# Two of the seven gate and value products, in the last two chunks, done as seven products of blocks of 128

## The chip, the cores and the metric

The kernel runs on one core of a Trainium2 chip. The metric is the device time of one execution in microseconds, as the median of several runs. One execution was also recorded by the hardware profiler; its times are measured from the start of its span.

## The reference

Attention with a threshold, followed by a SwiGLU block, all in float32. There are 8 batches of 8 heads, 576 positions, 64 columns a head.

```python
scores = scale * np.matmul(q, k.transpose(0, 1, 3, 2))
thresh = np.max(scores, axis=-1, keepdims=True) - tau
scores = np.where(scores >= thresh, scores, -1000000000.0)
attn = exp(scores - max); attn = attn / (sum(attn) + 1e-09)
x = (attn @ v) as (4608 tokens, 512)
g = x @ w_gate                       # 512 x 1536
silu = g * (1.0 / (1.0 + np.exp(-g)))
val = x @ w_val                      # 512 x 1536
return (silu * val @ w_out)          # 1536 x 512
```

## The kernel before

**Tokens and chunks.** The SwiGLU block works on chunks of 512 tokens. Chunks 0 to 7 are the first 512 positions of each batch, chunk 8 is the last 64 positions of all batches together. While the attention of batch c + 1 runs, its scores and softmax take turns with the SwiGLU steps of chunk c. After the last scores nothing is left but the end of chunk 6's output and chunks 7 and 8; this part is called the tail (`tail[0]` is true, L1833). There the sums that GpSimd does otherwise are VectorE's, and the four PSUM banks of the scores join the other four (`more_banks`, L1837).

**A group.** Gate and value of a chunk are made in 6 groups (g = 0 to 5) of 256 gate and 256 value columns. A group is one product of a 2 x 2 matrix of weight blocks by a 2 x 2 matrix of token blocks, each block 256 x 256: the halves of the inner dimension, gate against value, the two halves of the tokens. It is done with seven block products instead of eight, with sums and differences of blocks. Class `Group` (L923) has a method for each product, p1 to p7. Each calls `mul` (L935), four matmuls of 128x128 stationary weights by 128x256 tokens. They collect in the banks pa, pb and pe; ScalarE copies a bank between two products, or moves it to SBUF halved (L947, L963, L984, L1015). In p3, VectorE makes the first gate from pe and what ScalarE put aside (L1005); `finish` (L988) then has ScalarE make a tanh (L992) and VectorE two more steps (L993, and L798 for the last multiplication). `gates_and_values` (L1702) runs the groups; the order on TensorE is p1 of a group, p4 of the group before, then p5, p2, p6, p3, p7.

**Weights.** Sums of weights that were made early lie in HBM. For chunks from 2 on, each group's seven weight blocks come into one of two places in SBUF (`flow`, slot g % 2) in two loads, `load_flow` (L866 to L875): blocks 0 to 3 (1024 KB) and 4 to 6 (768 KB). The loads for group g + 2 are issued at the end of p6 (first part) and p4 (second part) of group g. Block 2 belongs to p5, block 5 to p3.

**Tokens.** `token_sums` (L888) makes the sums of token blocks. xs[0] is p5's, xs[2] is p3's.

**The output stage.** `Deep` (L1239) does the product with w_out in blocks, again with seven products. Its `nested` (L1302) splits five of them once more, each into seven products of three matmuls, 128x128 by 128x128, whose results lie in blocks of two banks in the order ORDER and at the places AT (L1299, L1300). Its sums are VectorE's in the tail (L798, shapes 128x512 and 128x384). `early` and part of the inner sums are made during groups 4 and 5, the rest while the stage runs. `combine` (L1338) adds the seven blocks into four, four adds in a row, from SBUF or from PSUM.

**The order of work.** A planner in the kernel's own code, class `Plan` (L28), fixes the order in which every engine gets its instructions. Each step is a job with an engine, an expected cost, the jobs it depends on, and a rank; TensorE's order is written out by hand, and the planner hands out the other engines' jobs in the order in which they would start. Once built, each engine's queue is strictly in that order, so an instruction that waits holds up all behind it.

Of the kernel before, what the change touches and what calls it, by code (L numbers as in the profile page):

```python
# [27 lines left out]
class Plan:  # L28
# [84 lines left out]
def kernel(  # L113
# [656 lines left out]
    def take(name, full=False):  # L770
        free = [b for b in banks if (not b.held if b.fixed is not None else b.n in turns)]
        if full:
            free = [b for b in free if b.full]
            return Hold(min(free, key=Bank.free_at), name) if free else None
        n = sum(b.full for b in free)
        return Hold(min(free, key=lambda b: (b.full and n == 1, max(b.free_at(), plan.t))), name)
# [20 lines left out]
    def dve_tt(out, a, b, op):  # L797
        return lambda: nc.vector.tensor_tensor(out=out, in0=a, in1=b, op=op)  # L798
# [89 lines left out]
    def token_sums(c, c2, deps, eng="POOL"):  # L888

        x11, x12, x21, x22 = (x_block(c, t, kh)[:, c2] for t in range(2) for kh in range(2))  # L890
        s1, s2, s4 = (x[:, c2] for x in xs)
        tt, took = (pool_tt, 0.75) if eng == "POOL" else (dve_tt, 0.36)
        j1 = job(eng, took, tt(s1, x21, x22, ALU.add), *deps, rank=0)
        j2 = job(eng, took, tt(s2, s1, x11, ALU.subtract), j1, rank=0)
        j4 = job(eng, took, tt(s4, x12, s2, ALU.subtract), j2, rank=0)
        j3 = job(eng, took, tt(x21, x11, x21, ALU.subtract), j1, rank=0)
        jobs = ready_x.setdefault(c, {n: [] for n in range(5)})
        for n, j in ((1, j1), (2, j2), (3, j3), (4, j4)):
            jobs[n].append(j)
        jobs[0] += deps  # L900
# [22 lines left out]
    class Group:  # L923
# [78 lines left out]
        def p3(self):  # L1002
            m = self.mul(self.e, self.w[5], xs[2], False, self.s5, *self.w_deps[5], *ready_x[self.c][4])
            u = self.u1_buf
            g1 = job("DVE", 0.7, lambda: nc.vector.scalar_tensor_tensor(out=u.ap, in0=self.e.rows(), scalar=0.5, in1=u.ap, op0=ALU.mult,  # L1005
                                                                        op1=ALU.add), m, self.u1, rank=0)
            self.e.read_by(g1)
            self.e.done(True)
            self.finish(0, u, g1, self.a, self.m2)
# [10 lines left out]
        def p4(self):  # L1020
            m = self.mul(self.b, self.w[4], x_block(self.c, 1, 1), False, self.u2, *self.w_deps[4])
            self.finish(1, self.u2_buf, self.g2, self.b, m)
            if self.g + 2 < NF2:
                if self.c < DEEP:
                    load_sums(self.c, self.g + 2, m)
                else:
                    load_flow(self.c, self.g + 2, 1, m)

    def plain_group(t, g, n_bufs):

        x = xts["full", t]

        def mul(mat, name):
            hold = take(name)

            def fn():
                ps = hold.rows()
                for i in range(2):
                    for c in range(NCC):
                        nc.tensor.matmul(ps[:, i], wgv[:, mat, c, (2 * g + i) * P:(2 * g + i + 1) * P], x[:, c, :],  # L1040
                                         start=(c == 0), stop=(c == NCC - 1))
# [197 lines left out]
    class Deep:  # L1239
# [62 lines left out]
        def nested(self, o, holds, first, *deps):  # L1302

            ws = weights_of(o)
            begun = set() if first else {0, 1}
            for n in self.ORDER:
                a, ready = self.inner[o][n]
                bank_, at_ = self.AT[n]

                def fn(n=n, a=a, bank_=bank_, at_=at_):  # L1310
                    ps = holds[bank_].ap()[:, at_ * P:(at_ + 1) * P]
                    for f in range(NF2 // 2):
                        nc.tensor.matmul(ps, a[:, f, :], ws[n][:, f, :], start=bank_ not in begun, stop=True, skip_group_check=True)  # L1313
                        begun.add(bank_)

                m = pe(0.67, fn, *ready, *deps, *deep_jobs[o])
            return m
# [384 lines left out]
    def gates_and_values(c):  # L1702

        old = None
        while u_bufs[0] is not u_list[0]:
            u_bufs.rotate(-1)
        for g in range(NF2):
            new = Group(c, g)
            new.p1(tail[0] or g not in (2, 4))
            yield  # L1710
            if old is not None:
                old.p4()
                if c >= DEEP and old.g == NF2 - 2:
# [12 lines left out]
        state["last_product"] = old.p4  # L1726
# [110 lines left out]
    def more_banks():  # L1837
        plan.force(*sc_users)
        for _ in range(2):
            ps = ps_s.tile([P, 2, 512], F32, name="sc")  # L1840
            for h in range(2):
                b_ = Bank(None, ps[:, h])
                banks.append(b_)

    more_banks()
    while state["run"]:
        out_steps(1)
    for c in (B - 1, B):
        for _ in gates_and_values(c):
            pass  # L1850
        begin_outputs(c)
        out_steps(2)
        if c < B:
            w = SM // 2
            j = []
            for kh in range(2):
                src = last_hbm[:, 2 * kh:2 * kh + 2, :].rearrange("p c (t n) -> p t c n", t=2)
                for t in range(2):
                    j.append(job("SP", 0.1, lambda kh=kh, t=t, src=src: nc.sync.dma_start(out=x_place(B, kh)[:, t], in_=src[:, t]),
                                 last_store[0], plan.t, lag=3.0))  # L1860
            for c2 in range(2):
                token_sums(B, c2, j, "DVE")
        while state["run"]:
            out_steps(1)
    plan.finish()


# [28 lines left out]
```

## Time and profile before

| | |
|---|---|
| median of 3 runs | 1383.91 us (1381.97 to 1387.38) |
| profiled execution | 1383.97 us |
| its span | 1382.1 us |
| granted TensorE clock, mean | 0.998 |
| busy over the span: PE, PEld, DVE | 1360.9 (98%), 1115.3 (81%), 1024.5 (74%) |
| busy over the span: ACT, POOL | 867.6 (63%), 701.2 (51%) |
| end of the last scores | 1141.5 us |
| first product of chunk 7, of chunk 8 | 1165.60, 1271.93 us |

The profile names an engine as PE (TensorE's matmuls), PEld (its weight loads), DVE (VectorE), ACT (ScalarE), POOL (GpSimd) or SP (SyncE, which issues the DMAs). A row shows the line of the code, what is written and read, the shape, and in brackets how long the engine stood idle before it and what released it. L798 is a helper that all two-operand sums on VectorE go through, L940 the matmuls of a group, L1313 the narrow ones of the output stage, L1322 its wide ones. The durations of matmuls overlap, so their pace is read from start to start.

### The profile page before, as it was taken

Reading aid. Unit: us, or ns where it says so; the run is one execution under the profiler, and the core shown is the slowest. Engines: PE = TensorE matmul, PEld = TensorE weight load, DVE = VectorE, ACT = ScalarE, POOL = GpSimd, SP = SyncE. Lnnn points to the kernel's source line nnn. Section 1 sums busy time; section 2 is a strip of 40 time slices with the busy share of each in tenths; the row PEclk is TensorE's granted clock in tenths of the full one; section 3 lists DMA queues with packets and bytes.
Section 4 is the critical chain, followed back from the end, with each engine's and each line's share of the span. In section 5 each row is a group of like instructions: output and inputs, shape, how many; then the busy total and the mean of one; then the engine's idle time right before and its main releaser. Section 6 shows DMA issues by size and latency. Waiting matters only on the chain.

```text
span 1382.1 us, 38805 instructions
## 1 busy us (share of the span) xinstructions
PE 1360.9 (98%) x15486; PEld 1115.3 (81%) x15486; DVE 1024.5 (74%) x2677; ACT 867.6 (63%) x2254; POOL 701.2 (51%) x649
## 2 busy tenths in 40 slices
PE   9988999999999999999999999999999999999998
PEld 6666787777778778887888888878887788889888
DVE  7978888887887777787778877877787764366355
ACT  6887766676755767767776766776767773220320
POOL 2456498844484669533974387437943592000000
PEclk9999999999999999999999999999999999999999
DMA  7733413465514541555154523553165404424411
GB/s 172 212 104 138 102 36 96 120 189 143 176 47 126 142 114 42 169 143 142 35 152 129 151 50 126 138 141 93 36 190 143 112 26 142 153 77 145 153 61 31
DMA packets 208291, 162.29 MB, mean 117 GB/s; under 512 B 166128, under 2 KB 180464, under 8 KB 202736
## 3 DMA queue, kind: packets, MB, share of 16 engines
q1 hardware_dynamic: 203920, 158.86, 40.7%
q8 instruction: 123, 2.02, 0.6%
q10 hardware_dynamic: 4192, 0.95, 0.3%
q14 instruction: 56, 0.46, 0.1%
HBM read 138.28 MB, written 21.50 MB: 116 GB/s over the span
## 4 chain that ended last, share of the span: by engine, by line
PE 91%; DVE 4%; ACT 2%; SPq 1%; DMA 1%; issue 1%; ACTq 0%; DVEq 0%
PE pb L940 17%; PE pa L940 12%; PE pe L940 12%; PE px L1313 12%; PE sc L1545 10%; PE xa L1642 9%; PE po L1109 5%; PE py L1322 5%; PE pg L1040 2%; PE pv L1040 2%; PE sc L940 1%; PE pv L517 1%; SPq L336 1%; PE xa L500 1%; PE sc L1313 1%
## 5 line engine op out<-in xcount | busy, mean ns | idle before, releaser
L1593 DVE SCALAR_TENSOR_TENSOR pall<-sc,th,pall 128x288 f32<-128x288 f32 x504 | 243.8, 514 | 63.6 <-ACT pall L1591 49.4
L940 PE MATMUL pb<-xall,big 128*128 128x256 f32 x1080 | 256.5, 380 | 0.0
L1591 ACT ACTIVATE pall<-sc,nm 128x288 f32<-128x288 f32 x504 | 232.0, 498 | 34.5 <-DVE pall L1593 34.2
L1621 DVE STREAM_TRANSPOSE pall<-pall 128x576 f32<-128x576 f32 x252 | 190.0, 765 | 59.4 <-ACT pall L1619 42.7
L940 PEld LDWEIGHTS pb<-xall,big 128*128 128x128 f32 x1080 | 203.7, 190 | 29.8 <-issue 2.2
L1619 ACT ACTIVATE pall<-pall,ri 128x288 f32<-128x288 f32 x408 | 186.8, 528 | 24.9 <-DVE ri L1607 24.3
L795 POOL TENSOR_TENSOR hall<-hall,tmp 128x512 f32<-128x512 f32 x80 | 103.7, 1296 | 160.2 <-DVE hall L993 144.8
L940 PE MATMUL pa<-xall,big 128*128 128x256 f32 x768 | 183.3, 381 | 0.0
L940 PE MATMUL pe<-xall,big 128*128 128x256 f32 x752 | 178.9, 381 | 0.0
L940 PEld LDWEIGHTS pa<-xall,big 128*128 128x128 f32 x768 | 144.0, 190 | 22.6 <-issue 2.7
L940 PEld LDWEIGHTS pe<-xall,big 128*128 128x128 f32 x752 | 141.9, 190 | 21.5 <-issue 2.7
L1545 PE MATMUL sc<-kT,qT 64*32 64x144 f32 (+1 forms) x5376 | 149.0, 345 | 3.4 <-DVE pall L1593 2.3
L1566 DVE TENSOR_REDUCE mx<-sc 128x2 f32<-128x576 f32 x168 | 124.8, 743 | 26.7 <-PE sc L1545 26.1
L1545 PEld LDWEIGHTS sc<-kT,qT 64*32 64x32 f32 x5376 | 97.5, 106 | 57.1 <-issue 21.1
L1642 PE MATMUL xa<-pall,vall 64*32 64x288 f32 x4032 | 132.2, 404 | 1.1 <-DVE hall L993 0.8
L1616 POOL TENSOR_SCALAR pall<-pall,ri 128x288 f32<-128x288 f32 x96 | 95.9, 1010 | 62.5 <-DVE ri L1607 62.4
L1642 PEld LDWEIGHTS xa<-pall,vall 64*32 64x32 f32 x4032 | 76.4, 107 | 50.2 <-issue 7.3
L1601 ACT COPY sums<-sums 32x6 f32<-32x6 f32 x336 | 66.7, 199 | 45.0 <-DVE pall L1593 40.5
L992 ACT ACTIVATE vall<-tmp 128x512 f32<-128x512 f32 x96 | 60.5, 630 | 52.6 <-DVE tmp L1005 29.9
L1580 ACT COPY mx<-mx 32x6 f32<-32x6 f32 x196 | 38.1, 195 | 61.3 <-DVE mx L1568 59.3
L1322 PE MATMUL py<-wo,hall 128*128 128x256 f32 x336 | 74.8, 379 | 0.0
L1568 DVE TENSOR_REDUCE mx<-sc 128x1 f32<-128x288 f32 x168 | 74.7, 445 | 0.0
(231 smaller groups left out, 2327.1 us busy)
## 6 DMA issues: line engine op xcount, KB each, us to landing
big<-sums_hbm SPq DMA_DIRECT2D x42, 1024.0 KB, 5.2
big<-sums_hbm SPq DMA_DIRECT2D x48, 768.0 KB, 4.8
vall<-in_v_dram SPq DMA_DIRECT2D x112, 144.0 KB, 3.0
out_dram<-big SPq DMA_DIRECT2D x32, 256.0 KB, 3.1
qT<-in_q_dram SPq DMA_DIRECT2D x112, 72.0 KB, 4.7
kT<-in_k_dram SPq DMA_DIRECT2D x112, 72.0 KB, 3.1
wo<-in_moe_w_gate_dram SPq DMA_DIRECT2D x16, 384.0 KB, 3.7
wo<-in_moe_w_val_dram SPq DMA_DIRECT2D x16, 384.0 KB, 4.5
```

The lines of the kernel that those rows point to most:

```text
L795: return lambda: nc.gpsimd.tensor_tensor(out=out, in0=a, in1=b, op=op)
L940: nc.tensor.matmul(ps[:, i], w[:, k_, i * P:(i + 1) * P], x[:, k_, :], start=first and i == k_ == 0, stop=True, skip_group_check=True)
L1313: nc.tensor.matmul(ps, a[:, f, :], ws[n][:, f, :], start=bank_ not in begun, stop=True, skip_group_check=True)
L1322: nc.tensor.matmul(ps(), a[:, f, i * P:(i + 1) * P], operands[o][:, f, :], start=first and f == 0, stop=True, skip_group_check=True)
L1545: nc.tensor.matmul(pss[h][(slice(g * G, (g + 1) * G), *part)], qT[hs, col:col + G], kT[hs, c * SH + keys[0]:c * SH + keys[1]], start=True, ...
L1566: rs.append(job("DVE", 0.72, lambda n=n, tile_=tile_: nc.vector.tensor_reduce(out=mx[:, n:n + 2, 0], in_=tile_[:, :, 0:SH], axis=AX.X, op= ...
L1591: ej = job("ACT", 0.42, lambda x=x, n=n: nc.scalar.activation(ps[x], scs[x], AF.Exp, bias=nm[:, n:n + 1]), ej, *((masks[h, 0], masks[h, 1] ...
L1593: masks[x] = job("DVE", 0.45, lambda x=x, n=n: nc.vector.scalar_tensor_tensor(out=ps[x], in0=scs[x], scalar=th[:, n:n + 1], in1=ps[x], op0 ...
L1616: scaled.append(job("POOL", 1.02, lambda x=x, n=n: nc.gpsimd.tensor_scalar(out=x, in0=x, scalar1=ri[:, n:n + 1], scalar2=None, op0=ALU.mul ...
L1619: scaled.append(job("ACT", 0.46, lambda x=x, n=n: nc.scalar.activation(x, x, AF.Copy, scale=ri[:, n:n + 1]), rj, rank=rank))
L1621: seg["turned"].append(job("DVE", 0.72, lambda both=both: nc.vector.transpose(out=both, in_=both), *scaled, rank=rank))
L1642: nc.tensor.matmul(holds[a].ap()[x * G:(x + 1) * G, 0:SH].rearrange("d (i q) -> d i q", q=G), vr[rs, h, j, ds], p[rs, h, :, j, :], start=( ...
```

## The change

In chunks 7 and 8 the groups are of a new class, `LateGroup`, with its own p5 and p3. Each of these two products is split once more into seven products, each one matmul of 128x128 weights by 128x128 tokens. ORDER and AT are those of the output stage. Two banks are taken instead of one.

- `deepen_weights` makes four sums of 128x256 (both products together) for the next group's weights on VectorE, after both of its loads. It is called in p5 of the group before, for group 0 during the output stage of the chunk before.
- `deepen_x` makes four sums of 128x256 of the tokens, once a chunk.
- After p5 ScalarE copies seven blocks to SBUF, halved (128x512 and 128x384, instead of one of 128x512), and `four_quarters` has VectorE add them into four, in four adds.
- After p3 ScalarE copies one block of 128x128 to SBUF and four_quarters adds from PSUM into SBUF. The gate step (L1005 before) then reads SBUF instead of PSUM.

```diff
+    def four_sums(places, a11, a12, a21, a22, *deps):
+        p1, p2, p3, p4 = places
+        j1 = job("DVE", 0.36, dve_tt(p1, a21, a22, ALU.add), *deps, rank=1)
+        j2 = job("DVE", 0.36, dve_tt(p2, p1, a11, ALU.subtract), j1, rank=1)
+        j4 = job("DVE", 0.36, dve_tt(p4, a12, p2, ALU.subtract), j2, rank=1)
+        return [j4, job("DVE", 0.36, dve_tt(p3, a11, a21, ALU.subtract), j4, rank=1)]
...
+    def deepen_x(c, *deps):
...
+        j = job("DVE", 0.36, dve_tt(t1, b12, b11, ALU.subtract), *deps, rank=1)
+        j = job("DVE", 0.36, dve_tt(t2, b22, t1, ALU.subtract), j, rank=1)
+        j = job("DVE", 0.36, dve_tt(t4, b21, t2, ALU.subtract), j, rank=1)
+        j = job("DVE", 0.36, dve_tt(t3, b22, b12, ALU.subtract), j, rank=1)
...
+    def four_quarters(place, q0, q1, one, *deps, psum=False):
...
+        if psum:
+            deps = [job("ACT", 0.28, lambda: nc.scalar.copy(y[:, 4:5], q0[:, 0:1]), *deps, rank=0)]
...
+        j = job("DVE", took, dve_tt(y[:, 0:2], twice(first), q0[:, 1:3], ALU.add), *deps, rank=rank)
+        j = job("DVE", took, dve_tt(y[:, 3:5], twice(y[:, 1:2]), q1[:, 1:3], ALU.add), j, rank=rank)
+        j = job("DVE", less, dve_tt(y[:, 1], y[:, 3], q0[:, 3], ALU.add), j, rank=rank)
+        return job("DVE", took, dve_tt(y[:, 2:4], twice(y[:, 4:5]), q1[:, 0:2], ALU.add), j, rank=rank)
...
+        ready = four_sums(places, a11, a12, a21, a22, loads[c, g, 0], loads[c, g, 1], *w_users[g % 2], plan.t + plan.PIPE)
...
+    class LateGroup(Group):
+        def nested(self, o, first, *deps):
...
+            def fn():
+                for n in ORDER:
+                    b_, at_ = AT[n]
+                    nc.tensor.matmul(self.es[b_].ap()[:, at_ * P:(at_ + 1) * P], wd[o][n], xd[o][n], start=b_ not in begun, stop=True,
+                                     skip_group_check=True)
+                    begun.add(b_)
...
+        def p5(self):
+            self.take_b()
+            self.es = [take("pe") for _ in range(2)]
+            m = self.nested(0, True, *(d for h in self.es for d in h.deps))
...
+            self.s5 = four_quarters(s_place, q0, q1, None, *self.c5, *old)
+            copy_jobs[0] = [self.s5]
+            if self.g + 1 < NF2:
+                deepen_weights(self.c, self.g + 1)
+
+        def p3(self):
+            m = self.nested(1, False, *self.c5, *ready_x[self.c][4])
...
+            j = four_quarters(e_place, self.es[0].ap(), self.es[1].ap()[:, 0:3 * P], None, m, *e_jobs[0], psum=True)
...
+            self.finish(0, u, g1, self.a, self.m2)
...
-            new = Group(c, g)
+            new = LateGroup(c, g) if tail[0] else Group(c, g)
...
+    deepen_x(B - 1, plan.t + plan.PIPE)
+    deepen_weights(B - 1, 0)
     while state["run"]:
         out_steps(1)
```

The second chunk of the tail has the same calls: `deepen_x(B)` after its token sums, and `deepen_weights(c + 1, 0)` in its output steps once its loads are planned.

More of the change, by code (lines that the diff above doesn't have):

```diff
@@ L1027, in p4 @@
                     load_flow(self.c, self.g + 2, 1, m)
+    ORDER = 0, 1, 3, 6, 4, 5, 2
+    AT = {0: (0, 0), 1: (0, 1), 5: (0, 2), 2: (0, 3), 3: (1, 0), 4: (1, 1), 6: (1, 2)}
+    end_ = SPARE + P + NF2 * TC
+    assert end_ + DM + P + 2 * GW <= OB + 2 * NCC * DFF + 2 * 3 * HW
+    copy_place, s_place = vall[:, 0:NQ * P], whole[:, end_:end_ + DM + P]
+    e_place = pall[:, PB * SH - DM - P:]
+    w_place = pall[:, PB * SH - DM - P - 4 * HW:PB * SH - DM - P].rearrange("p (s n o q) -> p s n o q", s=2, n=4, q=P)
@@ new lines @@
+    assert 4 * NQ * P + DM + 4 * HW + DM + P <= PB * SH
+    s_buf = Buf(s_place[:, 0:DM].rearrange("p (f n) -> p f n", n=TC))
+    copy_jobs, e_jobs = [[]], [[]]
+    w_users = [[], []]
+    x_deep = {}
+    def four_sums(places, a11, a12, a21, a22, *deps):
[4 more added lines that the diff above has]
+        return [j4, job("DVE", 0.36, dve_tt(p3, a11, a21, ALU.subtract), j4, rank=1)]
@@ new lines, in deepen_x @@
+    def deepen_x(c, *deps):
+        if "t" not in x_deep:
+            x_deep["t"] = [qkp.tile([P, S], F32, name=name)[:, 0:2 * HW // 2].rearrange("p (n o q) -> p n o q", n=2, q=P)
+                           for name in ("qT", "kT")]
+        t12, t34 = x_deep["t"]
+        x = xall[:, 3 * XW:3 * XW + 3 * HW].rearrange("p (o k n) -> p o k n", o=3, k=2)[:, 0:3:2]
+        b11, b12, b21, b22 = (x[:, :, k_, n * P:(n + 1) * P] for k_ in range(2) for n in range(2))
+        t1, t2, t3, t4 = t12[:, 0], t12[:, 1], t34[:, 0], t34[:, 1]
+        deps = *ready_x[c][1], *ready_x[c][4], *deps
+        j = job("DVE", 0.36, dve_tt(t1, b12, b11, ALU.subtract), *deps, rank=1)
+        j = job("DVE", 0.36, dve_tt(t2, b22, t1, ALU.subtract), j, rank=1)
+        j = job("DVE", 0.36, dve_tt(t4, b21, t2, ALU.subtract), j, rank=1)
+        j = job("DVE", 0.36, dve_tt(t3, b22, b12, ALU.subtract), j, rank=1)
+        x_deep[c] = [j], [(b11[:, o], b21[:, o], b22[:, o], t4[:, o], t1[:, o], t2[:, o], t3[:, o]) for o in range(2)]
@@ new lines, in four_quarters @@
+    def four_quarters(place, q0, q1, one, *deps, psum=False):
+        y = place.rearrange("p (x q) -> p x q", q=P)
+        q0, q1 = q0.rearrange("p (x q) -> p x q", q=P), q1.rearrange("p (x q) -> p x q", q=P)
+        took, less, rank = (0.42, 0.29, 0) if psum else (0.36, 0.23, 1)
+        if psum:
+            deps = [job("ACT", 0.28, lambda: nc.scalar.copy(y[:, 4:5], q0[:, 0:1]), *deps, rank=0)]
+        first = y[:, 4:5] if psum else q0[:, 0:1]
+        twice = lambda x: x.broadcast_to((P, 2, P))
+        j = job("DVE", took, dve_tt(y[:, 0:2], twice(first), q0[:, 1:3], ALU.add), *deps, rank=rank)
+        j = job("DVE", took, dve_tt(y[:, 3:5], twice(y[:, 1:2]), q1[:, 1:3], ALU.add), j, rank=rank)
+        j = job("DVE", less, dve_tt(y[:, 1], y[:, 3], q0[:, 3], ALU.add), j, rank=rank)
+        return job("DVE", took, dve_tt(y[:, 2:4], twice(y[:, 4:5]), q1[:, 0:2], ALU.add), j, rank=rank)
@@ new lines, with deepen_weights @@
+    late_sums = {}
+    def deepen_weights(c, g):
+        w = flow[:, g % 2 * GW:(g % 2 + 1) * GW].rearrange("p (o k f) -> p o k f", o=NQ, k=2)[:, 2:6:3]
+        a11, a12, a21, a22 = (w[:, :, k_, i * P:(i + 1) * P] for i in range(2) for k_ in range(2))
+        places = [w_place[:, g % 2, n] for n in range(4)]
+        ready = four_sums(places, a11, a12, a21, a22, loads[c, g, 0], loads[c, g, 1], *w_users[g % 2], plan.t + plan.PIPE)
+        s1, s2, s3, s4 = places
+        late_sums[c, g] = ready, [(a11[:, o], a12[:, o], s4[:, o], a22[:, o], s1[:, o], s2[:, o], s3[:, o]) for o in range(2)]
@@ new lines @@
+    class LateGroup(Group):
+        def nested(self, o, first, *deps):
+            begun = set() if first else {0, 1}
+            sums, wd = late_sums[self.c, self.g]
+            ready, xd = x_deep[self.c]
+            def fn():
[4 more added lines that the diff above has]
+                    begun.add(b_)
+            return pe(NQ * MM / 2, fn, *deps, *sums, *ready)
+        def p5(self):
+            self.take_b()
+            self.es = [take("pe") for _ in range(2)]
+            m = self.nested(0, True, *(d for h in self.es for d in h.deps))
+            q0, q1 = copy_place[:, 0:4 * P], copy_place[:, 4 * P:]
+            old, copy_jobs[0] = copy_jobs[0], []
+            self.c5 = [job("ACT", 0.57, lambda: nc.scalar.activation(q0, self.es[0].ap(), AF.Copy, scale=0.5), m, *old, rank=0),
+                       job("ACT", 0.46, lambda: nc.scalar.activation(q1, self.es[1].ap()[:, 0:3 * P], AF.Copy, scale=0.5), m, *old, rank=0)]
+            self.s = s_buf
+            old, s_buf.jobs = s_buf.jobs, []
+            self.s5 = four_quarters(s_place, q0, q1, None, *self.c5, *old)
[4 more added lines that the diff above has]
+            m = self.nested(1, False, *self.c5, *ready_x[self.c][4])
+            w_users[self.g % 2] = [plan.t + plan.PIPE]
+            y = e_place[:, 0:DM].rearrange("p (f n) -> p f n", n=TC)
+            j = four_quarters(e_place, self.es[0].ap(), self.es[1].ap()[:, 0:3 * P], None, m, *e_jobs[0], psum=True)
+            for h, full in zip(self.es, (True, False)):
+                h.read_by(j)
+                h.done(full)
+            u = self.u1_buf
+            g1 = job("DVE", 0.62, lambda: nc.vector.scalar_tensor_tensor(out=u.ap, in0=y, scalar=0.5, in1=u.ap, op0=ALU.mult, op1=ALU.add),
+                     j, self.u1, rank=0)
+            e_jobs[0] = [g1]
+            self.finish(0, u, g1, self.a, self.m2)
@@ L1862 @@
                 token_sums(B, c2, j, "DVE")
+            deepen_x(B)
         while state["run"]:
             out_steps(1)
+            if (c + 1, 0, 1) in loads and (c + 1, 0) not in late_sums:
+                deepen_weights(c + 1, 0)
     plan.finish()
```

## The prediction

> **What bounds the kernel now.** I read the chain of waits first, then the last 180 us in stretches of 20 us, then the timelines of TensorE and VectorE in that part, then the DMA issues. The change touches only chunks 7 and 8, from about 1165 us of the span on. The built order of both programs is the same on every engine up to there, and on SyncE and GpSimd it is the same to the end.
>
> The chain that ended last, shares of the span by engine:
>
> ```profile
> PE 91%; DVE 4%; ACT 2%; SPq 1%; DMA 1%; issue 1%; ACTq 0%; DVEq 0%
> ```
>
> Stretches of the end: length, busy time of PE, PEld, DVE, ACT, POOL, granted clock, DMA share, GB/s:
>
> ```profile
> 1220.00:1240.00 20.00, 20.00 (x110) 18.04 (x109) 14.78 (x26) 6.00 (x10) 0.00 (x0) 1.00 0.10 32
> ...
> 1280.00:1300.00 20.00, 20.00 (x95) 17.60 (x94) 8.11 (x12) 6.06 (x11) 0.00 (x0) 1.00 0.51 155
> 1300.00:1320.00 20.00, 20.00 (x94) 17.62 (x93) 6.22 (x10) 5.78 (x10) 0.00 (x0) 1.00 0.52 175
> ...
> 1340.00:1360.00 20.00, 20.00 (x155) 19.30 (x154) 15.83 (x30) 4.19 (x9) 0.00 (x0) 1.00 0.06 14
> ```
>
> TensorE has no gap at the full clock: 20.00 of 20. Nothing but matmul time sets the end here. VectorE has room in plain groups (6 to 8 of 20 us) and much less where the sums of the output stage fall in (14.8 and 15.8 of 20). GpSimd does nothing. What the change saves on TensorE is saved at the end, as long as VectorE, which gets all the new sums, is not late.
>
> The timeline of TensorE gives the price of both kinds of product (start, duration, each matmul recorded as two instructions):
>
> ```profile
> 1341.00 1.89 PE L940 MATMUL sc<-xall,big 128*128 128x256 f32 x8
> 1342.72 1.50 PE L1313 MATMUL px<-wo,hall 128*128 128x128 f32 x12
> 1344.06 0.83 PE L1313 MATMUL px<-big,hall 128*128 128x128 f32 x6
> 1344.73 0.83 PE L1313 MATMUL px<-wo,big 128*128 128x128 f32 x6
> 1345.40 1.50 PE L1313 MATMUL px<-big 128*128 128x128 f32 x12
> 1346.74 0.83 PE L1313 MATMUL px<-wo,big 128*128 128x128 f32 x6
> 1347.41 1.89 PE L940 MATMUL sc<-xall,big 128*128 128x256 f32 x8
> ```
>
> Start to start counts, not duration. The 41 products of L940 from 1271.93 to 1342.72 take 1.7266 us each: four matmuls of 256 columns, 0.4317 apiece. The 21 matmuls of 128 columns from 1342.72 to 1347.41 take 4.69 us, 0.2233 apiece.
>
> **TensorE, part by part.** p5 and p3 of each group drop 4 matmuls of 256 columns (1.727 us) and get 7 of 128 columns: 7 x 0.2233 = 1.563 us. Saved: 0.163 us. Two per group, 6 groups, 2 chunks: 24 x 0.163 = 3.9 us, all on the path. That is the most there is: 0.28% of the time. A rule speaks against it. The Trainium skill, TensorE: Matmul & The Clock Gate, section Back-to-back issue gap, gives for streams of weight load and matmul about 81 ns at 128 columns and 131 ns at 512, so that narrow matmuls lose most of their advantage to the load. Interpolated (my estimate) 256 columns would be 98 ns, seven narrow ones 567 against four wide ones 391: 45% dearer, 24 x 0.78 = 19 us lost. The rows of this float32 kernel say otherwise: half the columns cost 52% (0.2233 against 0.4317), loads included, with a new stationary block at each matmul. The deep output product is the same kind of stream, so I take the row. By the same page's section LDWEIGHTS a load of 128 columns takes 107 ns; at two per matmul, 14 x 0.107 = 1.49 us, the gain would be 24 x 0.23 = 5.6 us. I take that as the far end.
>
> **VectorE.** Prices: a 128x256 sum that depends on the one before starts 0.45 us after it (1249.23 to 1249.68), one that doesn't 0.34; 128x128 0.29 to 0.32. Added per group: the weights' four sums, 0.45 + 0.45 + 0.34 + 0.45 = 1.7; the four adds of four_quarters for p5 (from SBUF), 0.45 + 0.45 + 0.32 + 0.34 = 1.55; the same for p3 (PSUM), 1.55. Together 4.8 us, 58 us in 12 groups, and 1.5 us of token sums twice. All is put beside TensorE. A plain group has 12.1 us, of which VectorE works 6 x 0.69 = 4.1; with 4.8 it is 8.9 of 11.8: hidden. Cover gone, it would cost itself.
>
> The narrow place is the last two groups, where the output stage's sums (1.03 + 0.56 + 0.56 + 1.89 + 1.29 + 2.21 + 2.27 = 9.8 us of 128x512 and 128x384) stand among the group's own. The gaps that are left there before the change:
>
> ```profile
> 1224.24 0.69 DVE L993 SCALAR_TENSOR_TENSOR hall<-vall,pa 128x512 f32<-128x512 f32 x1 [0.70 <-ACT vall L992]
> ...
> 1228.03 0.69 DVE L993 SCALAR_TENSOR_TENSOR hall<-vall,pb 128x512 f32<-128x512 f32 x1 [1.77 <-PE pb L940]
> ...
> 1234.94 0.69 DVE L1005 SCALAR_TENSOR_TENSOR tmp<-pe,tmp 128x512 f32<-128x512 f32 x1 [0.36 <-PE pe L940]
> 1236.33 0.69 DVE L993 SCALAR_TENSOR_TENSOR hall<-vall,pa 128x512 f32<-128x512 f32 x1 [0.70 <-ACT vall L992]
> ...
> 1243.08 0.69 DVE L993 SCALAR_TENSOR_TENSOR hall<-vall,pb 128x512 f32<-128x512 f32 x1 [2.54 <-PE pb L940]
> ```
>
> I laid the built order of VectorE, ScalarE and TensorE out with these durations from 1160 us, each instruction behind its queue and its semaphores. (The same laying-out of the kernel before ends within 0.3 us of its span.) VectorE then works without a gap from about 1221 to 1244. The sums for the third part of the first output product end about 0.9 us before TensorE asks for them; the last group has no next weights to sum, which is what makes it fit. The next narrowest place is p7, which reads a copy that ScalarE makes while p3 runs: 0.9 us of margin before, 0.74 now that p3 is 0.16 shorter. Cost taken: nothing.
>
> The start of chunk 7 does not fit quite. The fourth token sum stands in VectorE's queue behind four adds of chunk 6:
>
> ```profile
> 1166.15 1.66 DVE L798 TENSOR_TENSOR big<-big,px 128x256 f32<-128x256 f32 x4 [2.91 <-ACT big L1350]
> ```
>
> They end at 1167.81, the sum at about 1168.2; p5 starts at 1167.33 and reads it with its fourth matmul at 1168.0. Cost: 0.2 us, once. At chunk 8 these sums stand in the output stage, 10 us or more ahead.
>
> **ScalarE** gets one more copy of p5's second bank (0.48) and a 128x128 copy before p3's adds (0.27): 3.6 + 0.75 us of 11.8 per group, idle 70%. The longer path from p3 to the gate (0.3 + 1.7 us) delays the release of pa's bank; TensorE has eight banks in this part and the next group uses others. Cost: nothing.
>
> **The added wait.** The weights' sums wait for the load of the next group's second half. Behind them on VectorE stand p3's adds, and behind those the gates and TensorE. A load that stands alone lands 4.3 to 5.3 us after issue; three together at the start of chunk 8 queue up:
>
> ```profile
> big<-sums_hbm SPq DMA_DIRECT2D x2, 1024.0 KB, 6.3
> big<-sums_hbm SPq DMA_DIRECT2D x1, 768.0 KB, 9.3
> ```
>
> In the groups the second half is issued at the end of p4, two products into a group, and lands 4.4 us later, about when p3 begins (p5, p2 and p6 take 5.0). The sums (1.7) then end 0.5 to 0.9 us before p3's adds can start (p3's 1.56, its end, a 0.27 copy). So nothing. The 9.3 us load is group 1's; its sums stand ahead of group 0's p5 adds, which can start about 3 us after it lands. The loads now also wait for those sums before they overwrite the weights; the sums lie a group earlier: nothing. SyncE's queue order is unchanged.
>
> **Sum.** -3.9 + 0.2 = -3.7 us. The profiled execution took 1383.97 us with a span of 1382.1; 1383.97 - 3.7 = 1380.3. It lies 0.06 us off the median shown, 1383.91: 1380.2 us. What the measurement of this kernel can tell from no change is about 0.5%, 6.9 us; the forecast lies within that.
>
> **Rivals.**
> 1. VectorE becomes the bound (slower). Place: the dense 15 us before the first output product of chunks 7 and 8. Point: from 6% longer durations there (0.9 of 15) TensorE waits; from some 18% the waits, 2 x (2.7 - 0.9) = 3.6 us, eat the gain; at 25% they are 2 x (3.75 - 0.9) = 5.7, +2 us: 1386. At 35% later sums are late in turn; I put +8, 1392. For it: 14.8 and 15.8 busy of 20 before anything is added. Against it: all shapes have rows here (0.42 for 128x256, SBUF or PSUM), and none varies by more than 3%.
> 2. The narrow matmuls don't run at L1313's rate: there three go to one place of PSUM, here each to another block. At 0.25 apiece the product is 1.75 us, the gain gone: 1384.4. Against it: L1313 also changes bank and block every third matmul with no sign of it.
> 3. The loads land late: by 1 us it costs nothing, by about 3.3 TensorE waits in most groups and the gain is gone, 1384. Against: the single loads of the groups vary by less than 1 us.
> 4. Weight loads alone set the rate: -5.4, 1378.5.
>
> **Chances.** Forecast (1379 to 1382) 0.70; no gain (2, 3) 0.13; slower by VectorE 0.11; the larger gain 0.06. The range takes in 4 and the case of no gain and most of 1: 1378.2 to 1386. Faster by over 0.5% (below 1377.0) 0.02: the whole sum doesn't reach it. Slower by over 0.5% (above 1390.8) 0.04. The rest 0.94.
>
> **What would show it.** Right: TensorE busy 20.00 of 20 between 1170 and 1370; the seven of a product 1.56 us from start to start; a group 11.76 us instead of 12.08; VectorE near 9 us of a group, full in the last two; the first output product of chunk 7 at about 1234.7 instead of 1236.4. Wrong: a TensorE wait for VectorE at the first output product, or for the weights' sums in p5; seven matmuls taking 1.7 us or more.

## The result and the profile after

| | before | after |
|---|---|---|
| median of the runs | 1383.91 us (1381.97 to 1387.38) | 1379.78 us (1378.96 to 1381.42) |
| profiled execution | 1383.97 us | 1379.44 us |
| its span | 1382.1 us | 1377.3 us |
| busy PE | 1360.9 us (98%) | 1356.8 us (99%) |
| busy DVE | 1024.5 us (74%) | 1081.5 us (79%) |

The medians differ by 4.1 us. The ratio of the two, over all runs, is 0.9973 with an interval of 0.9963 to 0.9982: 3.7 us less, between 2.5 and 5.1. Run again later beside other runs of the kernel before, it gave 1379.66 us and a ratio of 0.9980 (0.9971 to 0.9989), 2.8 us less, between 1.5 and 4.0. The forecast of 3.7 us less lies in both intervals. That the forecast of 1380.2 us fell within 0.4 of the median is partly luck: the runs of one kernel scatter by more than 2 us.

**A finer measure for 3.7 us.** The spans of the two profiled executions differ by 4.8 us, but not all of that is the change. Up to the last output product of chunk 6 the two programs have the same instructions, and yet this product starts at 1160.81 us before and at 1159.64 after. Over the ten profiled executions of this study that start lies anywhere from 1158.46 to 1160.81, and no instruction ahead of it differs. A part of this goes with the clock: the four that start latest (1160.17 to 1160.81, the kernel before among them) have a granted clock of 0.96 between 40 and 80 us, the other six (1158.46 to 1159.81) 1.00 there. So I compare the time from this start to the end of the span, and call it the tail: 1382.1 - 1160.81 = 221.29 us before, 1377.3 - 1159.64 = 217.66 after, that is 3.63 less. In the second run of the changed kernel it is 217.69. The experiments below are all read by it.

First the chain that ended last, of the changed kernel:

```profile
PE 91%; DVE 4%; ACT 2%; SPq 1%; DMA 1%; issue 1%; ACTq 0%; DVEq 0%
```

It has the same shares as before: TensorE still sets the end. The stretches of the changed kernel say the same (length, busy time of PE, PEld, DVE, ACT, POOL, granted clock, DMA share, GB/s):

```profile
1180.00:1200.00 20.00, 20.00 (x114) 18.18 (x113) 14.76 (x32) 7.21 (x14) 0.00 (x0) 1.00 0.54 180
1220.00:1240.00 20.00, 20.00 (x130) 18.55 (x129) 19.16 (x38) 7.31 (x14) 0.00 (x0) 1.00 0.05 14
1280.00:1300.00 20.00, 20.00 (x117) 18.24 (x116) 14.56 (x30) 7.39 (x14) 0.00 (x0) 1.00 0.43 139
1340.00:1360.00 20.00, 20.00 (x152) 19.17 (x151) 16.00 (x30) 3.53 (x8) 0.00 (x0) 1.00 0.06 14
```

TensorE is busy 20.00 of 20 at the full clock in all four. VectorE has gone from 8.1 to 14.6 in plain groups (1280 to 1300) and from 14.8 to 19.2 in the last groups of chunk 7 (1220 to 1240): nearly full, and TensorE doesn't show it. The fourth stretch doesn't cover the same work in both kernels.

The gain itself is on TensorE's timeline (start, duration, line). This is one product of the new kind and the start of the next group's:

```profile
1178.23 0.61 PE L1101 MATMUL pe<-xall,big 128*128 128x128 f32 x4
1178.67 0.39 PE L1101 MATMUL sc<-kT,big 128*128 128x128 f32 x2
1178.89 0.39 PE L1101 MATMUL sc<-kT,pall 128*128 128x128 f32 x2
1179.12 0.39 PE L1101 MATMUL sc<-qT,pall 128*128 128x128 f32 x2
1179.34 0.39 PE L1101 MATMUL pe<-qT,pall 128*128 128x128 f32 x2
1179.56 0.39 PE L1101 MATMUL pe<-xall,pall 128*128 128x128 f32 x2
1179.79 1.89 PE L940 MATMUL pa<-xall,big 128*128 128x256 f32 x8
...
1189.99 0.61 PE L1101 MATMUL pe<-xall,big 128*128 128x128 f32 x4
```

From 1178.23 to 1179.79 the seven narrow matmuls take 1.56 us, where four wide ones took 1.727. From 1178.23 to 1189.99 a whole group takes 11.76, where seven products of 1.7266 took 12.09. In the column behind the operation one sees the matmuls change between the two banks (pe and sc) without any gap; that each goes to another block of its bank follows from AT in the code.

### The profile page after: what moved, and what is told of

It reads as the page before. It is cut to its first block, busy times and chain, and to the rows that moved or that the text cites. A ratio compares the mean times of both kernels' runs of the same rounds, so it can differ in the third digit from the quotient of the medians.

```text
span 1377.3 us, 39288 instructions
## 1 busy us (share of the span) xinstructions
PE 1356.8 (99%) x15630; PEld 1116.4 (81%) x15630; DVE 1081.5 (79%) x2829; ACT 875.1 (64%) x2278; POOL 700.2 (51%) x649
## 3 DMA queue, kind: packets, MB, share of 16 engines
q8 instruction: 124, 2.03, 0.6%
## 4 chain that ended last, share of the span: by engine, by line
PE 91%; DVE 4%; ACT 2%; SPq 1%; DMA 1%; issue 1%; ACTq 0%; DVEq 0%
PE pb L940 18%; PE pa L940 12%; PE px L1420 12%; PE sc L1652 10%; PE xa L1749 9%; PE pe L940 9%; PE po L1216 5%; PE py L1429 5%; PE sc L1101 2%; PE pg L1147 2%; PE pv L1147 2%; PE pv L517 1%; PE pe L1101 1%; SPq L336 1%; PE xa L500 1%
## 5 line engine op out<-in xcount | busy, mean ns | idle before, releaser
L940 PE MATMUL pb<-xall,big 128*128 128x256 f32 x1152 | 273.5, 380 | 0.0
L940 PEld LDWEIGHTS pb<-xall,big 128*128 128x128 f32 x1152 | 216.4, 190 | 31.0 <-issue 2.2
L940 PE MATMUL pe<-xall,big 128*128 128x256 f32 x576 | 137.3, 381 | 0.0
L940 PEld LDWEIGHTS pe<-xall,big 128*128 128x128 f32 x576 | 108.4, 190 | 17.0 <-issue 2.7
```

What stands on the lines that cost most here:

```text
L940: nc.tensor.matmul(ps[:, i], w[:, k_, i * P:(i + 1) * P], x[:, k_, :], start=first and i == k_ == 0, stop=True, skip_group_check=True)
```

## The experiments

| | tail, us | against before | against after | median, us | ratio to before |
|---|---|---|---|---|---|
| before | 221.29 | | +3.63 | 1383.91 | |
| after | 217.66 | -3.63 | | 1379.78 | 0.9973 (0.9963 to 0.9982) |
| after, again | 217.69 | -3.60 | +0.03 | 1379.66 | 0.9980 (0.9971 to 0.9989) |
| an eighth matmul | 223.24 | +1.95 | +5.58 | 1385.57 | 1.0019 (1.0010 to 1.0028) |
| the sums alone | 221.27 | -0.02 | +3.61 | 1383.25 | 0.9999 (0.9990 to 1.0008) |
| four more sums | 220.03 | -1.26 | +2.37 | 1383.51 | 1.0005 (0.9996 to 1.0014) |
| eight more sums | 227.47 | +6.18 | +9.81 | 1390.44 | 1.0058 (1.0044 to 1.0071) |
| late sums | 232.45 | +11.16 | +14.79 | 1394.72 | 1.0085 (1.0071 to 1.0099) |
| chunk 8 alone | 219.28 | -2.01 | +1.62 | 1381.32 | 0.9989 (0.9980 to 0.9998) |
| fourth token sum first | 217.40 | -3.89 | -0.26 | 1379.16 | 0.9974 (0.9963 to 0.9984) |

Each ratio is to runs of the kernel before on the same chip: their median was 1383.91 us for the first row after, 1382.50 for the eighth matmul, the sums alone, the four more sums and the late sums, and 1382.80 for the others.

My theory was the prediction's: TensorE's matmul time alone sets the end, so the gain is 24 products by 0.163 us, and all the new sums lie beside it. The rival was that the gain has another size at its source, and that part of it is taken back by a wait: then adding or leaving out matmuls would not give their full price, or leaving the sums out would give some time back.

### An eighth narrow matmul in each product

Each of the 24 products does one more matmul, into a block of the second bank that nobody reads. Neither VectorE nor ScalarE gets more work.

```diff
                     begun.add(b_)
+                nc.tensor.matmul(self.es[1].ap()[:, 3 * P:4 * P], wd[o][0], xd[o][0], start=False, stop=True, skip_group_check=True)
-            return pe(NQ * MM / 2, fn, *deps, *sums, *ready)
+            return pe((NQ + 1) * MM / 2, fn, *deps, *sums, *ready)
```

> The changed kernel with an eighth narrow matmul in each of the 24 split products, into the block of the second bank that nobody reads. Nothing else is different. Theory (the whole gain is TensorE's pace, 0.2233 us a matmul of 128 columns): 24 x 0.2233 = 5.4 us longer than the changed kernel, that is 1.3 to 1.6 us longer than the kernel before (8 x 0.2233 = 1.786 against 1.727 a product, plus the 0.2 us at the start of chunk 7). Rival (the gain comes from elsewhere, so that TensorE has room in the split products): it stays near the changed kernel, 3 to 4 us below the kernel before.

The tail grew by 5.58 us; 24 x 0.2233 gives 5.36. Up to the first output product of chunk 8 it grew by just 5.36; the rest came later, in chunk 8's output stage, where nine narrow matmuls take 2.18 us instead of 2.01. The timeline of TensorE, eighth matmul (L1104) included:

```profile
1177.48 0.61 PE L1101 MATMUL pe<-xall,big 128*128 128x128 f32 x4
...
1178.82 0.39 PE L1101 MATMUL pe<-xall,pall 128*128 128x128 f32 x2
1179.05 0.39 PE L1104 MATMUL sc<-xall,big 128*128 128x128 f32 x2
1179.27 1.89 PE L940 MATMUL pa<-xall,big 128*128 128x256 f32 x8
```

The eight take 1179.27 - 1177.48 = 1.79 us, and the eighth 0.22. With it the product is dearer than the four wide matmuls were (1.727), and the whole kernel is slower than before. So a matmul's time counts in full in these products, and the edge of the change is narrow: seven pay, eight don't.

### The sums alone

p5 and p3 are done with the four wide matmuls again. All the sums of the change are still made on VectorE (tokens, weights, and both four_quarters, here from SBUF), but nobody uses them; ScalarE has its old copy.

```diff
         def p5(self):
-            self.take_b()
-            self.es = [take("pe") for _ in range(2)]
-            m = self.nested(0, True, *(d for h in self.es for d in h.deps))
...
+            super().p5()
+            copy_jobs[0] = [four_quarters(s_place, q0, q1, None, self.s5, *copy_jobs[0])]
...
         def p3(self):
-            m = self.nested(1, False, *self.c5, *ready_x[self.c][4])
+            m = self.mul(self.e, self.w[5], xs[2], False, self.s5, *self.w_deps[5], *ready_x[self.c][4])
...
+            j = four_quarters(e_place, q0, q1, None, m, *e_jobs[0])
```

> p5 and p3 are wide as before, four matmuls of 256 columns, but VectorE makes all that the change adds as well: the token sums, the weights' sums after their loads, four adds after p5 and four ahead of p3's gate; nobody uses the results. Theory (VectorE's 61 us lie beside TensorE's work): the same as the kernel before within 0.5 us, TensorE busy without a gap. Rival (VectorE's sums cost something that the gain hides): longer than the kernel before by 1 us or more, with waits of TensorE at the end of chunk 7's groups.

The tail is that of before, 221.27 against 221.29, and the whole times agree (ratio 0.9999). Its stretches, columns as above:

```profile
1220.00:1240.00 20.00, 20.00 (x112) 18.09 (x111) 19.47 (x40) 6.08 (x10) 0.00 (x0) 1.00 0.07 22
1340.00:1360.00 20.00, 20.00 (x156) 19.28 (x155) 18.53 (x37) 4.06 (x8) 0.00 (x0) 1.00 0.06 14
```

VectorE works 19.5 of 20 us and TensorE 20.00. 54 us more work of VectorE (1078.4 us busy against 1024.5) cost nothing. Together with the run before it this splits the result: the matmuls give 3.6 us, the sums take none of it. What this run leaves out is that in the changed kernel p3's adds read PSUM and hold two banks meanwhile; the next two runs bear on that.

### Four and eight more sums at the narrow place

How near was VectorE to being the bound? In the last group of each chunk, ahead of p3's four adds, VectorE makes four more sums of 128x512 that nobody uses. Their cost in the planner is 0, so the order of all else stays.

```diff
-            j = four_quarters(e_place, self.es[0].ap(), self.es[1].ap()[:, 0:3 * P], None, m, *e_jobs[0], psum=True)
+            more = m
+            for _ in range(4 if self.g == NF2 - 1 else 0):
+                more = job("DVE", 0.0, dve_tt(e_place[:, 0:DM], copy_place[:, 0:DM], copy_place[:, 0:DM], ALU.add), m, more, *e_jobs[0], rank=0)
+            j = four_quarters(e_place, self.es[0].ap(), self.es[1].ap()[:, 0:3 * P], None, m, more, *e_jobs[0], psum=True)
```

> The changed kernel with four idle 128x512 sums (0.61 us each, 2.4 us) ahead of p3's adds in the last group of chunks 7 and 8, in an otherwise unchanged order of all queues. In the changed kernel p3's adds of chunk 7's last group end about 0.7 us before TensorE writes the bank that they read (as the first split output product's second bank). Theory (the reserve is that 0.7 us, and beyond it every microsecond counts): TensorE waits 1.7 to 1.9 us at that place in chunk 7; in chunk 8 the output product takes another bank and nothing waits; 1.8 us longer than the changed kernel, still about 2 us below the kernel before. Rival (VectorE has no reserve there): 2.4 us in each chunk, 4.8 us longer, slower than the kernel before by 0.7. Rival (room to spare): no change.

In the changed kernel itself, VectorE's last add of p3 in chunk 7 and TensorE's first matmul that writes the same bank again (sc) stand like this; first VectorE:

```profile
1233.81 0.42 DVE L798 TENSOR_TENSOR pall<-pall,sc 128x256 f32<-128x256 f32 x1
```

and TensorE:

```profile
1233.57 1.50 PE L1420 MATMUL px<-wo,hall 128*128 128x128 f32 x12
1234.91 0.83 PE L1420 MATMUL sc<-big,hall 128*128 128x128 f32 x6
```

The add ends at 1233.81 + 0.42 = 1234.23, TensorE wants the bank at 1234.91: 0.68 us of reserve. With the four sums, the timeline of TensorE has:

```profile
1234.10 1.50 PE L1423 MATMUL px<-wo,hall 128*128 128x128 f32 x12
1237.47 0.94 PE L1423 MATMUL sc<-big,hall 128*128 128x128 f32 x6 [1.87 <-DVE pall L798]
```

and that of VectorE the four sums:

```profile
1232.53 2.86 DVE L798 TENSOR_TENSOR pall<-vall 128x512 f32<-128x512 f32 x4
```

TensorE waits 1.87 us at that very matmul in chunk 7 and nowhere in chunk 8, as expected. The four sums are dearer than I had reckoned: the next sum starts at 1235.31, 2.78 us after the first of them and not 2.4, since each was made to follow the one before. Counted from the tail's start, the last add comes 2.66 us later than in the changed kernel; the reserve of 0.68 goes off, 1.98 is left. A wait in brackets counts from the end of the matmul before, and that end overlaps the next start by some 0.16 us; from start to start (1234.10 to 1237.47, 3.37 for 1.34) the pause costs 2.03. The three matmuls behind it take 0.77 instead of 0.67. The tail grew by 2.37. Of the 0.24 that are left, 0.19 lie in chunk 8's output stage, between 1355.73 and 1361.77 (6.04 us instead of 5.85), where the profile names no wait.

The whole time does not show the gain that remains: the median of 1383.51 lies among runs of 1380.89 to 1387.31, while I had expected some 2 us less than before. The tail of its profile is 1.26 less than before, which the interval of the ratio (from 0.6 us less to 1.9 more) doesn't hold; the place and the wait rest on the profile alone. Five of the eleven executions, the slowest ones, had a mean granted clock of 0.996 or 0.997, the profiled one 0.999; of the changed kernel's 22 executions two had 0.997. Whether the pause took the clock down in those five is not shown.

The same edit with eight sums instead of four:

> The changed kernel with eight idle 128x512 sums (4.9 us) ahead of p3's adds in the last group of chunks 7 and 8. Theory: chunk 7 waits 4.9 - 0.7 = 4.2 us and some tenths to get going again; chunk 8, whose output product has banks of its own, has a reserve of about 2.3 us until its own sums are late, and waits 2.6 us: 7 to 7.5 us longer than the changed kernel, 3.5 to 4 us longer than the kernel before. Rival (chunk 8 has no reserve either): 9 us or more longer. Rival (only chunk 7 has the narrow place): 4.5 us longer.

The tail grew by 9.81, not by 7 to 7.5. By the number alone that is the first rival (9 us or more, no reserve in chunk 8); the waits say otherwise. Its timeline of TensorE:

```profile
1239.24 1.36 PE L1423 MATMUL sc<-big,hall 128*128 128x128 f32 x6 [4.78 <-DVE pall L798]
1240.39 1.49 PE L1423 MATMUL sc<-wo,big 128*128 128x128 f32 x6
1241.67 1.47 PE L1423 MATMUL sc<-big 128*128 128x128 f32 x6
1242.95 0.86 PE L1423 MATMUL px<-big 128*128 128x128 f32 x6
...
1352.74 1.60 PE L1423 MATMUL px<-wo,hall 128*128 128x128 f32 x12 [2.16 <-ACT pall L1445]
```

The waits are 4.78 in chunk 7 and 2.16 in chunk 8 (and one of 0.22). The second wait names a copy on ScalarE, but that isn't late by itself; ScalarE's timeline shows what it stood behind:

```profile
1350.98 1.23 ACT L992 ACTIVATE vall<-tmp 128x512 f32<-128x512 f32 x2 [6.18 <-DVE tmp L1134]
1352.12 0.57 ACT L1445 COPY pall<-px 128x512 f32<-128x512 f32 x1
```

The copy stands behind two tanh that waited 6.18 us for the gate step (L1134) on the delayed VectorE. In chunk 8 the sums have no bank to hold up in time, and a strict queue passes the delay on by another engine. The eight sums take 5.68 us in chunk 7 (1231.39 to 1237.07) and 5.69 in chunk 8, not 4.9. From start to start TensorE's pause in chunk 7 costs 4.94 (1232.96 to 1239.24 for 1.34), and in chunk 8 it loses 2.91 (1348.69 to 1356.01, 7.32 for 4.41). So chunk 8 does have a reserve, 5.69 - 2.91, some 2.8 us. Most of what is left is the clock. The stretches of this run from the pause on (columns as above, the granted clock is third from the end):

```profile
1236.00:1239.00 3.00, 0.00 (x0) 0.00 (x0) 2.86 (x7) 0.00 (x0) 0.00 (x0) 1.00 0.00 0
1239.00:1242.00 3.00, 2.76 (x14) 2.76 (x15) 2.84 (x6) 1.23 (x2) 0.00 (x0) 0.60 0.00 0
1242.00:1245.00 3.00, 3.00 (x22) 2.92 (x22) 2.90 (x7) 0.48 (x1) 0.00 (x0) 0.83 0.00 0
1245.00:1248.00 3.00, 3.00 (x24) 2.87 (x23) 2.41 (x5) 0.48 (x2) 0.00 (x0) 1.00 0.18 59
```

After the pause of 4.78 us the clock is 0.60 and then 0.83 before it is full again. Three narrow matmuls take 1240.39 to 1241.67 = 1.28 us instead of 0.67, about half the pace. From 1239.24 to 1243.65 twelve narrow matmuls take 4.41 us instead of 2.68: 1.73 lost. With the same 0.19 in chunk 8's output stage as in the run before, 4.94 + 1.73 + 2.91 + 0.19 = 9.77 of the 9.81. The wait of 1.87 in the run with four sums and that of 2.16 here were followed by no such slow stretch.

### Late sums

In the program the load of the second half of the next group's weights stands behind p2 instead of behind the p4 before it, and so do the four weight sums of the next group. It was meant to make both 3.3 us late.

```diff
             copy_jobs[0] = [self.s5]
+
+        def p4(self):
+            m = self.mul(self.b, self.w[4], x_block(self.c, 1, 1), False, self.u2, *self.w_deps[4])
+            self.finish(1, self.u2_buf, self.g2, self.b, m)
+
+        def p2(self):
+            super().p2()
+            if 1 <= self.g < NF2 - 1:
+                load_flow(self.c, self.g + 1, 1, self.m2)
             if self.g + 1 < NF2:
                 deepen_weights(self.c, self.g + 1)
```

> The changed kernel, but the second half of the next group's weights is asked for at the end of p2 instead of at the end of the p4 before it, 3.3 us later (1.56 + 1.73), and the weights' sums with it. Theory (the added wait is covered by less than 2 us): TensorE waits for the sums in p5 of groups 2 to 5, about 1.7 us each time, 8 x 1.7 = 13 us; 13 us longer than the changed kernel and 9 to 10 us longer than the one before. What the prediction said of loads 3.3 us late: 4 us longer than the changed kernel, level with the kernel before. Rival (the load is covered by a whole group): no change.

The loads did not come later. In the changed kernel this p4 runs from 1176.50 to 1178.23, and SyncE issues the load then:

```profile
1178.42 0.34 SPq L873 DMA_DIRECT2D big<-sums_hbm  x1
```

Here p4 runs from 1177.20 to 1178.93, p2 to 1182.22, and the load is issued behind p4 all the same:

```profile
1179.12 0.34 SPq L873 DMA_DIRECT2D big<-sums_hbm  x1
```

The deferred place in the program made no instruction wait for p2. Only the sums moved, because the planner reckons with a later load. No sum on VectorE waits for a load in this run, where in the changed kernel seven do.

TensorE waits in 8 groups, 1.6 us each, as the waits of this run sum them up (us, number, longest):

```profile
PE sc L1101 <- DVE pall L798: 12.6, 8, 1.6
```

One of them on TensorE's timeline, at the fourth matmul of p5, the one that reads the last of the sums:

```profile
1191.13 0.39 PE L1101 MATMUL sc<-kT,big 128*128 128x128 f32 x2
1193.10 0.49 PE L1101 MATMUL sc<-kT,pall 128*128 128x128 f32 x2 [1.58 <-DVE pall L798]
1193.42 0.39 PE L1101 MATMUL sc<-qT,pall 128*128 128x128 f32 x2
```

and the sums on VectorE:

```profile
1188.30 0.42 DVE L798 TENSOR_TENSOR pall<-big 128x256 f32<-128x256 f32 x1
...
1190.56 0.42 DVE L798 TENSOR_TENSOR pall<-pall,big 128x256 f32<-128x256 f32 x1
...
1192.29 0.42 DVE L798 TENSOR_TENSOR pall<-big,pall 128x256 f32<-128x256 f32 x1
1192.63 0.42 DVE L798 TENSOR_TENSOR pall<-big 128x256 f32<-128x256 f32 x1
```

The tail grew by 14.79, a little more than the 13 expected. From start to start the shown wait costs 1.97 - 0.22 = 1.75, and the matmul behind it comes after 0.32 instead of 0.22: 1.85 a group, 14.8 in eight. The four sums take 4.7 us from first to last where they would take 1.7: they now stand in the queue among gate steps that wait for other things, and the last of them comes 7.9 us later than in the changed kernel, counted from the tail's start. So the run shows what sums that stand that late in VectorE's queue cost. That its number came near the expected one, which was worked out for late loads, is luck. What late loads would cost was not tried.

### Chunk 8 alone

Only chunk 8 gets the new class, chunk 7 is done as before.

```diff
-            new = LateGroup(c, g) if tail[0] else Group(c, g)
+            new = LateGroup(c, g) if c == B else Group(c, g)
...
-    deepen_x(B - 1, plan.t + plan.PIPE)
-    deepen_weights(B - 1, 0)
```

> The change in chunk 8 alone; chunk 7's p5 and p3 are wide as before. Theory: half the products, 12 x 0.163 = 2.0 us shorter than the kernel before, and no wait for the token sums (that one is chunk 7's). From chunk 6's last output product to the end 219.3 us (221.3 in the kernel before, 217.7 in the changed one). Rival (the gain is a matter of one chunk, or of what stands ahead of them): the whole 3.7 us, or nothing.

The tail is 2.01 us shorter than before: 12 x 0.163 = 1.96. The other 3.63 - 2.01 = 1.62 is chunk 7's: the same 1.96 less the 0.3 us that it loses at its start (next section). So the change is worth in one chunk what it is worth in the other.

### The fourth token sum first

```diff
-        j = job("DVE", 0.36, dve_tt(t3, b22, b12, ALU.subtract), j, rank=1)
+        j = job("DVE", 0.36, dve_tt(t3, b22, b12, ALU.subtract), j, rank=0)
```

> The changed kernel with the fourth token sum given the first rank, so that in VectorE's queue it stands ahead of the four adds of chunk 6's last output product instead of behind them. Theory: TensorE's wait of 0.2 us in chunk 7's first p5 goes, and nothing else moves: 0.2 us, 217.4 to 217.5 us from chunk 6's last output product to the end, which the time of the whole cannot tell from the changed kernel. Rival: those adds, now 0.3 us later, hold up the store or the bank, and the 0.2 us are given back.

In the changed kernel the sum stood behind four adds of chunk 6 on VectorE,

```profile
1164.99 1.66 DVE L798 TENSOR_TENSOR big<-big,px 128x256 f32<-128x256 f32 x4 [0.90 <-ACT big L1457]
1166.56 0.42 DVE L798 TENSOR_TENSOR kT<-xall 128x256 f32<-128x256 f32 x1
```

and TensorE's fourth matmul came 0.42 us after the third instead of 0.22:

```profile
1166.16 0.61 PE L1101 MATMUL pe<-xall,big 128*128 128x128 f32 x4
1166.61 0.39 PE L1101 MATMUL sc<-kT,big 128*128 128x128 f32 x2
1167.03 0.49 PE L1101 MATMUL sc<-kT,pall 128*128 128x128 f32 x2
1167.36 0.39 PE L1101 MATMUL sc<-qT,pall 128*128 128x128 f32 x2
```

The matmul after the pause is late as well, 0.33 us behind it instead of 0.22, so that the pause costs 0.20 + 0.11 = 0.31 us.

With the first rank the planner puts it ahead of them; VectorE now:

```profile
1162.97 0.41 DVE L798 TENSOR_TENSOR kT<-xall 128x256 f32<-128x256 f32 x1
1163.95 1.65 DVE L798 TENSOR_TENSOR big<-big,px 128x256 f32<-128x256 f32 x4 [0.56 <-ACT big L1457]
```

and TensorE:

```profile
1165.57 0.39 PE L1101 MATMUL sc<-kT,big 128*128 128x128 f32 x2
1165.79 0.39 PE L1101 MATMUL sc<-kT,pall 128*128 128x128 f32 x2
1166.01 0.39 PE L1101 MATMUL sc<-qT,pall 128*128 128x128 f32 x2
```

Both gaps are 0.22 and the tail is 0.26 us shorter. The rival, that the gain is given back elsewhere, is not borne out. The whole time of 1379.16 us is the lowest of all, but 0.2 us is far below what the runs can tell from the changed kernel's 1379.66 in the same session. That this version is better rests on the profile.

### The changed kernel again

It ran beside the last three, to have its time and its tail twice.

> The changed kernel once more, beside the others on one chip. Theory: 3.7 us shorter than the kernel before, as the sum of the prediction has it, 217.7 us from chunk 6's last output product to the end. If the 4.1 us of the first comparison hold more than the sum: 4 us or more shorter again.

Its tail is 217.69 against 217.66, so a tail can be read to about 0.1 us. That is what made differences of 0.2 to 2 us legible, which whole times don't show. The whole time is 2.8 us less than before by the ratio, not 4 or more: the 4.1 between the first two medians held scatter.

## Why the prediction was right

**TensorE, -3.9 us.** Right in size and cause. The seven take 1.56 us as summed, the group 11.76. The eighth matmul and the change in chunk 8 alone move TensorE's work by what the rows say. Before the change chunk 8's first output product, behind the last of the 24 products, started at 1342.72, 181.91 us into the tail. Now it is:

```profile
1337.94 1.50 PE L1420 MATMUL px<-wo,hall 128*128 128x128 f32 x12
```

That is 178.30 us into the tail, 3.61 less; with the 0.31 us that chunk 7's start costs, 3.92: the 24 x 0.163 of the sum.

**The rule that spoke against it.** It would have made the kernel 19 us slower; it became 3.6 us faster. The row of the same kind of stream (0.2233 us for 128 columns against 0.4317 for 256) held in the new place. So it didn't matter that each matmul goes to another block of PSUM (second rival), and the rate is not that of the weight loads alone (fourth rival): PEld is busy 18.2 of 20 us where PE is 20.00, and the gain isn't 5.4. The page's formula had a load at 107 ns; in the profile before, the loads of L1313 are 192 ns long, two to a matmul, and a matmul starts every 223 ns. So the recorded loads overlap, and their length doesn't give the pace.

**Chunk 7's start, +0.2 us.** Right in place, a little small: the pause is the 0.20 that I had, and the late start of the matmul behind it, which I had not reckoned with, adds 0.11. It is the only pause of TensorE for the new work, and moving the sum shortens the tail by 0.26.

**VectorE, nothing.** Right. It works 14.76 of 20 us in plain groups, 14.76 x 11.76 / 20 = 8.7 a group, where I had said near 9, and 19.2 of 20 in the last two of chunk 7. The experiment with the sums alone shows that they take nothing.

**The reserve at the output stage.** The size was near, 0.68 us for 0.9, but I named the wrong thing. It isn't the sums for the third part of the product that would be late first, it is a bank: p3's adds read PSUM directly, and the second matmul group of the output stage writes that bank again. And chunk 8 has no such place, which my formula for the first rival (twice what exceeds the reserve of 0.9) had: with four more sums it has no wait. Taken for added sums, 2.78 us in each chunk, the formula gives 3.8 us, and the tail grew by 2.4. For 5.68 us it gives 9.6, and the tail grew by 9.8, but that is luck: chunk 7 pays 6.7 of it, 1.7 of them by the clock, and chunk 8 2.9.

**The added wait for the loads, nothing.** Right for the kernel as it is: the wait shows on VectorE and not on TensorE. On VectorE's timeline of the changed kernel one looks so:

```profile
1218.26 0.43 DVE L798 TENSOR_TENSOR pall<-big 128x256 f32<-128x256 f32 x1 [0.56 <-DMA big<-sums_hbm]
```

There are 7 such waits from 1160 us on, 4.4 us in all, and each ends in time. Whether loads 3.3 us later would take back the gain, as my third rival had it, stays open: the run that was to show it moved only the sums. It does show what I had left out, that sums which stand late in VectorE's queue cost far more than the gain, 14.8 us.

**p7, ScalarE, other banks, nothing.** No wait of TensorE shows up at any of them. ScalarE's share I summed wrongly: 3.6 + 0.75 of 11.8 us leaves it idle 63%, not 70, and it works 7.2 to 7.4 of 20 us in plain groups.

**The first output product of chunk 7.** Predicted at 1234.7, it started at 1233.57, but this execution was 1.17 us ahead before the change began: 1233.57 + 1.17 = 1234.74.

## What to carry to other kernels

Where TensorE has no gap, price a change of its matmuls from start to start in rows of the same type and stream, multiply by the count, and ask of every other engine only whether it stays in time. Lay the queues out in order and look for the least reserve: here it was 0.68 us at a bank that a later product reuses, not at any operand. To judge a gain of 0.3% measure from the last point where both programs are the same; what lies ahead of it scatters by more than half of the gain.

## What I had not expected of the hardware

A pause of TensorE can cost much more than its length: after 4.78 us the granted clock was 0.60 and 0.83 in the next two stretches of 3 us, some 1.7 us more, while pauses of 1.6 to 2.2 us in the profiled executions cost only about 0.1 more. Where between these lengths it begins, no run here shows. The Trainium skill (TensorE: Matmul & The Clock Gate, section Part 1: The HAM clock gate) has the clock fall to half after an idle window of about 3.4 us; both kinds of pause agree with that, and so does the halved pace after the long one.
